# Attention and two feed-forward layers on one core: emission priorities, a longer unordered stretch on ScalarE, and the last output by row blocks

## The chip, the cores and the metric

The kernel runs on one core of a Trainium2 chip. The metric is the time of one execution on the device in microseconds (us), the median of several runs; smaller is better. TensorE (PE in the profile) multiplies matrices, VectorE (DVE) and ScalarE (ACT) work elementwise, GpSimd (POOL) does almost nothing here, and SyncE (SP) issues the transfers (DMAs).

## What is computed

Batch 4, 8 heads, 576 positions, head size 64. Four heads attend to the last 32 positions, four to every 32nd earlier position. The result, 2304 tokens by 512, goes through two feed-forward layers, each 512 to 2048 to 512.

```python
attn = softmax(where(mask, q @ k.T / 8, -1e9))        # heads 0-3: local, heads 4-7: strided
x = (attn @ v).reshape(2304, 512)
h = np.maximum(x @ w_in, 0.0);  x = h * h @ w_out      # first layer
h = x @ w_in2;  g = np.maximum(h, 0) + alpha * np.minimum(h, 0)
out = g @ w_out2                                       # second layer
```

## The kernel before, in words

**Steps.** The two feed-forward layers are a list of 208 steps (layer, tile, f): f counts the 16 blocks of 128 hidden units. Layer 0 has seven tiles of tokens. Tiles 0 to 2 have 256 columns and take steps 0 to 47 (0 to 31 for tiles 0 and 1 in a mixed order, 32 to 47 for tile 2); tiles 3 to 6 have 384 columns and take steps 48 to 111. Layer 1 has six tiles of 384, steps 112 to 207.

**One step.** Every fp32 operand is split into a high part and a low rest, so one product is three products. `emit_h` makes 12 matmuls into one PSUM bank, `ps_h` (line 566). `emit_g` makes the activation on ScalarE: in layer 0 `g` by Relu (L578), `gh`, its square rounded to the short format (L579), and the full square (L580). `emit_gl` subtracts the two on VectorE and gives the rest `gl` (L594). `emit_y` adds 12 matmuls (9 in layer 1) into the output banks `ps_y` (L620): those on `gh` first, those on `gl` last. There is a single `ps_h` bank, so the matmuls of h(n+1) wait until Relu (L578) has read h(n).

**Beside the steps** other work is laid into the list: the conversion of the weights from the 64-bit words in which they arrive (L159, L162, L185 on ScalarE, L171 to L191 on VectorE); the units of local attention (class `Unit`: scores L245, mask and maximum L259 and L263, exponentials L267, scaling L274 to L282, transpose L289 and its copy L293, values L299, output L308 and L315); and strided attention (class `Strided`), which is almost all VectorE work: products L450 and L491, sums L457 and L498. The first two tiles have attention of their own beside (class `Dense`, L340 to L400).

**The order.** Within `run` a step is written as `gl(n)`, h(n+1), attention and conversions, `g(n+1)`, y(n). A framework then orders each engine. Engines named in `manual_schedule` keep the written order; the others get the order in which a scheduler, which estimates when every instruction can start, would pick them by priority, and on the chip each engine then runs its list in that fixed order. SyncE is manual throughout; ScalarE only in the second of two stretches, which begins at step 32. TensorE and VectorE are never manual:

```python
        emit_h(0)
        emit_g(0)
        run(range(2 * NF))
    with tc.manual_schedule(engines={mybir.EngineType.SP, mybir.EngineType.Activation}):
        run(range(2 * NF, len(steps)))
```

**The buffer e.** A unit's masked scores and exponentials lie in `e`, of which there is one for all units from tile 2 on (`bufs=1`, L255). **The end.** `evac` (L625) copies the three output banks of a tile of layer 1 into SBUF, the first and third on ScalarE (L641), the second on VectorE (L643), and SyncE stores each 128 x 512 block (L645).

Of the kernel before, what the change touches and what calls it, by code (L numbers as in the profile page):

```python
# [10 lines left out]
AF = mybir.ActivationFunctionType  # L11
# [5 lines left out]
P = 128  # L17
# [5 lines left out]
NTILE = 6  # L23
# [47 lines left out]
def attn_moe_moe2(  # L71
# [37 lines left out]
    nc = tc.nc  # L109
    NT, DM = out.shape  # L110
    NF = w_in1.shape[0]
    NC = DM // P
    T = NT // NTILE
# [94 lines left out]
    class Unit:  # L208


        bufs = None
# [40 lines left out]

        def softmax_a(self):
            n = self.n
            self.e = self.new("e", [P, 3, 96], bufs=1)[:, 0:n]  # L255
            self.st = apool.tile([P, 3, 4], F32, tag="st", name="stat", bufs=4)[:, :, 0:n]
            s = self.s[:, 0:96 * n].rearrange("p (n c) -> p n c", c=96)
            m = mfirst if self.first else mloc
            nc.vector.scalar_tensor_tensor(  # L259
                out=self.e, in0=s, scalar=SCALE,  # L260
                in1=m.unsqueeze(1).to_broadcast([P, n, 96]), op0=ALU.mult, op1=ALU.add,
            )
            nc.vector.tensor_reduce(out=self.st[:, 0, :], in_=self.e, op=ALU.max, axis=AX.X, negate=True)  # L263
# [284 lines left out]
    steps = [(0, t, f) for t, f in FIRST]  # L548
# [3 lines left out]
    g_sb, y_ps, ybank, hs = {}, {}, {}, {}  # L552
# [38 lines left out]
    def emit_gl(n):  # L591
        g, gh = g_sb[n]
        gl = gpool.tile([P, T], F32R, tag="gl", name="gl")[:, 0:cols_of(n)]
        nc.vector.tensor_tensor(  # L594
            out=gl, in0=g, in1=gh.bitcast(F32), op=ALU.subtract
        )
        g_sb[n] = (gh, gl)

    def emit_y(n):
        l, t, f = steps[n]  # L600
        gh, gl = g_sb.pop(n)
        w = wslot[l, f]
        no = NC if l == 0 else NSUB
        if f == 0:
            for o in range(no):
                if (l, t) != (0, 1):
                    ybank[o] = psum(f"y{o}")
                first = COLS[0] if (l, t) == (0, 1) else 0
                y_ps[l, t, o] = ybank[o][:, first:first + (cols_of(n) if l == 0 else DM)]
        for part in range(2):  # L610
            for o in range(no):
                y = y_ps[l, t, o]
                sl = slice(o * P, (o + 1) * P)
                if l == 0:
                    ops = ((w[:, 2, sl], gh), (w[:, 3, sl], gh), (w[:, 2, sl], gl))
                else:
                    ops = ((gh[:, sl], w[:, 2, :]), (gh[:, sl], w[:, 3, :]), (gl[:, sl], w[:, 2, :]))
                for i, (a, b) in enumerate(ops):
                    if (i == 2) == (part == 1):
                        nc.tensor.matmul(  # L620
                            y, a, b, start=(f == 0 and i == 0 and (l, t) != (0, 1)),
                            stop=(f == NF - 1 and i == 2), skip_group_check=(l == 0 and t < 2),
                        )

    def evac(t, layer):  # L625
        no = NC if layer == 0 else NSUB
        cols = COLS[t] if layer == 0 else DM
        if layer == 0:
            y1[t] = dpool.tile([P, NC, cols], F32, tag=f"y1_{t}", name=f"y1_{t}")
        tags = (("so", 2, 1), ("wt", 2, 2)) if layer == 0 else (("so", 1, 1), ("sq", 1, 1), ("wt", 1, 2))  # L630
        if layer == 0 and t < 2:
            tags = (("wt", 2, 2),) * 2
        evs = []
        for tag, per, bufs in tags:
            ev = spool.tile([P, per, cols], F32, tag=tag, name="ev", bufs=bufs)
            evs += [ev[:, i, :] for i in range(per)]
        for o in range(no):
            ev = evs[o]
            y = y_ps.pop((layer, t, o))
            if o % 2 == 0 or layer == 0:  # L640
                nc.scalar.activation(out=ev, in_=y, func=AF.Copy)  # L641
            else:
                nc.vector.tensor_copy(ev, y)  # L643
            dst = y1[t][:, o, :] if layer == 0 else out[t * T + o * P:t * T + (o + 1) * P, :]
            nc.sync.dma_start(out=dst, in_=ev)  # L645
# [107 lines left out]
    def run(ns):  # L753
        for n in ns:
            l, t, f = steps[n]
            emit(starts, n)
            emit(loads, n)
            emit_gl(n)
            emit(front, n)
            if n + 1 < len(steps):  # L760
                emit_h(n + 1)
            emit(fill, n)
            emit(tensor_part, n)
            if n + 1 < len(steps):
                emit_g(n + 1)
            emit(tail_part, n)
            emit_y(n)
            if f == NF - 1:
                evac(t, l)

    outs = {}
    with tc.manual_schedule(engines={mybir.EngineType.SP}):
# [7 lines left out]
        bufs = {}  # L780
        for t, tags in enumerate((("w7", "w8", "w9", "w10"), ("w15", "w14", "w13", "w12"))):
            n = D * (t + 1)
            a = part(tags[0], 640, 640, 384, 384)
# [55 lines left out]
                fn(*args)  # L839
        emit_h(0)  # L840
        emit_g(0)
        run(range(2 * NF))
    with tc.manual_schedule(engines={mybir.EngineType.SP, mybir.EngineType.Activation}):
        run(range(2 * NF, len(steps)))


_OUTS = [((2304, 512), "float32")]
# [104 lines left out]
```

## Time and profile before

| | us |
|---|---|
| median of 3 runs (894.0 to 895.51) | 895.06 |
| the profiled execution | 895.83 |
| its span, first to last instruction | 894.0 |
| TensorE busy | 870.4 (97%) |
| VectorE busy | 553.5 (62%) |
| ScalarE busy | 455.1 (51%) |

The profiled execution stands 1.8 us above its span. A share over the whole span is a mean over very different stretches: at the start the transfers of weights fill the DMA engines, then VectorE is full with strided attention and weight conversion, and from about 200 us on TensorE has no gap until the last step.

### The profile page before, as it was taken

The numbers are of one execution on the slowest core, as the hardware profiler recorded it, in microseconds if no ns is written. First come the engines' busy times: TensorE is split into PE (matmuls) and PEld (weight loads), VectorE is DVE, ScalarE is ACT, GpSimd is POOL, SyncE is SP. The second block draws the span as 40 slices with busy tenths as digits, with TensorE's granted clock in tenths as the row PEclk, the third lists the DMA queues.
The fourth block names the chain that finished last, engine by engine and source line by source line (L and its number), as shares of the span: only waits on it lengthen the run. The fifth ranks groups of instructions, "written<-read, shape, count | busy, mean of one in ns | idle before, by whom it ended". The sixth has DMA issues, their size and how long they took to land.

```text
span 894.0 us, 13787 instructions
## 1 busy us (share of the span) xinstructions
PE 870.4 (97%) x5448; PEld 817.4 (91%) x5448; DVE 553.5 (62%) x877; ACT 455.1 (51%) x1063; POOL 1.5 (0%) x10
## 2 busy tenths in 40 slices
PE   6799999899999999999999999999999999999997
PEld 5699989799999999999999999999999999999996
DVE  5999999949678796794598983233233333333322
ACT  6889655455545554545577664334334334334332
POOL 0000000000000000000000000000000000000000
PEclk9999999999999999999999999999999999999999
DMA  9990402111212212100687200100100100100000
GB/s 295 393 339 2 153 8 86 45 52 62 71 51 73 68 56 73 49 8 26 241 271 267 82 10 27 36 9 29 34 10 30 33 10 30 33 9 32 5 1 36
DMA packets 33537, 70.34 MB, mean 79 GB/s; under 512 B 5696, under 2 KB 17600, under 8 KB 33472
## 3 DMA queue, kind: packets, MB, share of 16 engines
q1 hardware_dynamic: 33472, 69.46, 22.8%
q8 instruction: 43, 0.70, 0.3%
q14 instruction: 22, 0.18, 0.1%
HBM read 60.01 MB, written 9.44 MB: 78 GB/s over the span
## 4 chain that ended last, share of the span: by engine, by line
PE 88%; DMA 6%; DVE 4%; ACT 1%; issue 1%; SPq 0%; ACTq 0%; DVEq 0%
PE ps_y L620 42%; PE ps_h L566 42%; DMA wraw<-in_w1o_dram 2%; DMA att_w<-in_qd_dram 1%; PE ps_o L299 1%; PE ps_s L245 1%; DMA wraw<-in_w1i_dram 1%; DMA att_w<-in_v_dram 1%; PE ps_pt L289 1%; DVE pr L491 1%; DVE ss L457 1%; DVE w L191 0%; DVE so L498 0%; DVE pr L450 0%; DVE gl L594 0%
## 5 line engine op out<-in xcount | busy, mean ns | idle before, releaser
L566 PE MATMUL ps_h<-xh_c,w 128*128 128x384 f32 (+1 forms) x896 | 221.5, 316 | 4.6 <-ACT g L578 4.2
L566 PE MATMUL ps_h<-xh,w 128*128 128x384 f32 x768 | 212.5, 337 | 0.0
L585 DVE SCALAR_TENSOR_TENSOR g<-u,nalpha,g 128x384 f32<-128x384 f32 x96 | 59.3, 618 | 193.9 <-ACT u L584 193.9
L594 DVE TENSOR_TENSOR gl<-g,gh 128x384 fp32r<-128x384 f32 (+1 forms) x208 | 108.6, 523 | 107.8 <-ACT g L580 57.9
L566 PEld LDWEIGHTS ps_h<-xh_c,w 128*128 128x128 f32 x896 | 157.9, 191 | 7.1 <-ACT g L578 5.4
L620 PE MATMUL ps_y<-gh,w 128*128 128x384 f32 (+1 forms) x896 | 158.3, 319 | 0.0
L620 PE MATMUL ps_y<-w,gh 128*128 128x512 f32 x576 | 149.0, 394 | 0.1
L566 PEld LDWEIGHTS ps_h<-xh,w 128*128 128x128 f32 x768 | 140.4, 188 | 4.2
L566 PE MATMUL ps_h<-xl_c,w 128*128 128x384 f32 (+1 forms) x448 | 140.7, 314 | 0.0
L620 PEld LDWEIGHTS ps_y<-gh,w 128*128 128x128 f32 x896 | 138.7, 190 | 1.5
L583 ACT ACTIVATE g<-ps_h 128x384 f32<-128x384 f32 x96 | 47.2, 492 | 168.5 <-PE ps_h L566 168.2
L566 PE MATMUL ps_h<-xl,w 128*128 128x384 f32 x384 | 128.9, 336 | 0.0
L578 ACT ACTIVATE g<-ps_h 128x384 f32<-128x384 f32 (+1 forms) x112 | 49.4, 441 | 151.2 <-PE ps_h L566 146.6
L620 PEld LDWEIGHTS ps_y<-w,gh 128*128 128x128 f32 x576 | 106.6, 188 | 17.2 <-ACT gh L588 0.6
L620 PE MATMUL ps_y<-gl,w 128*128 128x384 f32 (+1 forms) x448 | 86.2, 313 | 2.0 <-DVE gl L594 1.9
L566 PEld LDWEIGHTS ps_h<-xl_c,w 128*128 128x128 f32 x448 | 85.5, 191 | 0.1
L588 ACT ACTIVATE gh<-g 128x384 fp32r<-128x384 f32 x96 | 50.5, 526 | 68.1 <-DVE g L585 68.1
L620 PE MATMUL ps_y<-w,gl 128*128 128x512 f32 x288 | 82.0, 392 | 0.0
L566 PEld LDWEIGHTS ps_h<-xl,w 128*128 128x128 f32 x384 | 72.1, 188 | 4.1
L620 PEld LDWEIGHTS ps_y<-gl,w 128*128 128x128 f32 x448 | 71.7, 189 | 2.6 <-DVE gl L594 2.6
L620 PEld LDWEIGHTS ps_y<-w,gl 128*128 128x128 f32 x288 | 54.1, 188 | 12.5
L579 ACT ACTIVATE gh<-g 128x384 fp32r<-128x384 f32 (+1 forms) x112 | 53.8, 480 | 2.9
(98 smaller groups left out, 840.7 us busy)
## 6 DMA issues: line engine op xcount, KB each, us to landing
wraw<-in_w1i_dram SPq DMA_DIRECT2D x16, 512.0 KB, 8.8
wraw<-in_w1o_dram SPq DMA_DIRECT2D x16, 512.0 KB, 9.1
wraw<-in_w2i_dram SPq DMA_DIRECT2D x16, 512.0 KB, 3.7
wraw<-in_w2o_dram SPq DMA_DIRECT2D x16, 512.0 KB, 4.7
qk<-in_qk_dram SPq DMA_DIRECT2D x16, 336.0 KB, 3.8
out_dram<-ev SPq DMA_DIRECT2D x18, 256.0 KB, 2.3
y<-ev SPq DMA_DIRECT2D x16, 192.0 KB, 2.0
x2raw<-y SPq DMA_DIRECT2D x16, 192.0 KB, 3.2
```

The source lines that it names most:

```text
L245: nc.tensor.matmul(s, self.qk[:, j, 0:P], self.qk[:, j, P:], start=True, stop=True)
L289: nc.tensor.transpose(self.pt_ps[0:96, P * j:P * j + P], self.e[:, j, :], ident)
L299: nc.tensor.matmul(self.o[64 * h:64 * h + 64, 64 * j:64 * j + 64], self.v[:, j, D * h:D * h + D], self.pt[:, P * j + 64 * h:P * j + 64 * h ...
L457: nc.vector.tensor_reduce(out=self.s[:, b, r:r + ROWS, j0:j1], in_=pr, op=ALU.add, axis=AX.X)
L566: nc.tensor.matmul(h[:, 0:b.shape[2]], a, b[:, c, :], start=(c == 0 and i == 0), stop=(c == NC - 1 and i == 2))
L578: nc.scalar.activation(out=g, in_=h, func=AF.Relu)
L579: nc.scalar.activation(out=gh, in_=g, func=AF.Square)
L583: nc.scalar.activation(out=g, in_=h, func=AF.Relu)
L585: nc.vector.scalar_tensor_tensor(out=g, in0=u, scalar=nalpha[:, f:f + 1], in1=g, op0=ALU.mult, op1=ALU.add)
L588: nc.scalar.activation(out=gh, in_=g, func=AF.Copy)
L594: nc.vector.tensor_tensor(out=gl, in0=g, in1=gh.bitcast(F32), op=ALU.subtract)
L620: nc.tensor.matmul(y, a, b, start=(f == 0 and i == 0 and (l, t) != (0, 1)), stop=(f == NF - 1 and i == 2), skip_group_check=(l == 0 and t ...
```

## The change

Five edits. (1) `e` gets two buffers. (2) `emit_gl(n)` and `emit_g(n+1)` are put under high priority, which the scheduler uses on every engine that it orders. (3) ScalarE's manual stretch begins at step 48 and no longer at step 32, and SyncE's two manual stretches meet there too. (4) In the last step of all, the nine matmuls of y are sorted by output block. (5) In the last tile the second and third output block are copied in two halves, left on VectorE and right on ScalarE, and each half is stored by itself, left from SyncE, right from ScalarE's queue.

```diff
-            self.e = self.new("e", [P, 3, 96], bufs=1)[:, 0:n]
+            self.e = self.new("e", [P, 3, 96], bufs=2)[:, 0:n]
...
-        for part in range(2):
-            for o in range(no):
...
+        order = [(part, o) for part in range(2) for o in range(no)]
+        if n == len(steps) - 1:
+            order.sort(key=lambda x: x[1])
+        for part, o in order:
...
+            if layer == 1 and t == NTILE - 1 and o > 0:
+
+                rows, half = slice(t * T + o * P, t * T + (o + 1) * P), DM // 2
+                nc.vector.tensor_copy(ev[:, 0:half], y[:, 0:half])
+                nc.sync.dma_start(out=out[rows, 0:half], in_=ev[:, 0:half])
+                nc.scalar.activation(out=ev[:, half:], in_=y[:, half:], func=AF.Copy)
+                nc.scalar.dma_start(out=out[rows, half:], in_=ev[:, half:])
+                continue
...
-            emit_gl(n)
+            with tc.high_priority():
+                emit_gl(n)
...
-                emit_g(n + 1)
+                with tc.high_priority():
+                    emit_g(n + 1)
...
-        run(range(2 * NF))
+        run(range(3 * NF))
...
-        run(range(2 * NF, len(steps)))
+        run(range(3 * NF, len(steps)))
```

In the program as built, ScalarE's copy of a right half waits for VectorE's copy of the left half of the same PSUM bank.

Three places show how the order moves; numbers behind names are the framework's, so the same tile may have another one before and after. First VectorE between `gl` of step 25 (`gl_1628`) and of step 26 (`gl_1672`), before:

```order
L594 TENSOR_TENSOR gl_1628<-g_1602,gh_1603 128x256
L457 TENSOR_REDUCE ss_1524<-pr_1587 128x2x5
L315 TENSOR_TENSOR xl_c2_1132<-ps_o_1594,xh_c2_1131 128x128
L450 TENSOR_TENSOR pr_1646<-kv_1440,sq_1482 128x640
L450 TENSOR_TENSOR pr_1648<-kv_1440,sq_1482 128x768
L457 TENSOR_REDUCE ss_1524<-pr_1646 128x2x5
L457 TENSOR_REDUCE ss_1524<-pr_1648 128x2x6
L191 TENSOR_TENSOR w0_15_1630<-wt_1591,w0_15_1630 128x2x512
L594 TENSOR_TENSOR gl_1672<-g_1653,gh_1654 128x256
```

and after the change:

```order
L594 TENSOR_TENSOR gl_1628<-g_1602,gh_1603 128x256
L457 TENSOR_REDUCE ss_1524<-pr_1585 128x2x8
L259 SCALAR_TENSOR_TENSOR e_1608<-ps_s_1599,mloc_79 128x192
L450 TENSOR_TENSOR pr_1587<-kv_1440,sq_1482 128x640
L594 TENSOR_TENSOR gl_1672<-g_1653,gh_1654 128x256
```

Three pieces stand between the two instead of seven; the products, sums and the weight conversion `w0_15` come behind `gl_1672`.

Second ScalarE around steps 36 and 37, before. `g_2095` and `g_2146` are Relu of steps 36 and 37, `e_2058` the second local unit of tile 3, whose exponentials (L267) need the maximum `stat_2059` from VectorE:

```order
L578 ACTIVATE g_2095<-ps_h_2076 128x256
L579 ACTIVATE gh_2096<-g_2095 128x256
L580 ACTIVATE g_2095<-g_2095 128x256
L267 ACTIVATE e_2058,stat_2059<-e_2058,stat_2059 128x96 x3
L282 ACTIVATE e_2058<-e_2058,stat_2059 128x96 x3
L578 ACTIVATE g_2146<-ps_h_2117 128x256
```

and after, where the same unit is `e_2055`, the first unit `e_1957`, and Relu of steps 36 and 37 `g_2092` and `g_2143`:

```order
L267 ACTIVATE e_2055,stat_2056<-e_2055,stat_2056 128x96
L282 ACTIVATE e_1957<-e_1957,stat_1958 128x96 x3
L578 ACTIVATE g_2092<-ps_h_2073 128x256
L267 ACTIVATE e_2055,stat_2056<-e_2055,stat_2056 128x96
L579 ACTIVATE gh_2093<-g_2092 128x256
L267 ACTIVATE e_2055,stat_2056<-e_2055,stat_2056 128x96
L580 ACTIVATE g_2092<-g_2092 128x256
L578 ACTIVATE g_2143<-ps_h_2114 128x256
```

The six instructions that stood between the squares of step 36 and Relu of step 37 are gone from there: the exponentials are spread around step 36, and the scalings L282 of that unit come behind the squares of step 37.

Third ScalarE at step 1, before. `g_470` is Relu of that step, `att_w13_90` the copy of a transpose of dense attention for tile 1, `w0_2` and `wraw` are weight conversion, `xh_c1` the high part of tile 1:

```order
L578 ACTIVATE g_470<-ps_h_453 128x256
L375 ACTIVATE att_w13_90<-ps_pt_491 128x512
L579 ACTIVATE gh_471<-g_470 128x256
L159 ACTIVATE wraw_120<-wraw_120 128x1024
L185 ACTIVATE w0_2_408<-wt_377 128x512 x2
L580 ACTIVATE g_470<-g_470 128x256
L394 ACTIVATE xh_c1_513<-ps_o_412 128x512
```

and after:

```order
L578 ACTIVATE g_470<-ps_h_453 128x256
L267 ACTIVATE att_w15_88,stat_393<-att_w15_88,stat_393 128x96
L579 ACTIVATE gh_471<-g_470 128x256
L267 ACTIVATE att_w15_88,stat_393<-att_w15_88,stat_393 128x96
L580 ACTIVATE g_470<-g_470 128x256
L267 ACTIVATE att_w15_88,stat_393<-att_w15_88,stat_393 128x96 x2
L159 ACTIVATE wraw_120<-wraw_120 128x1024
L185 ACTIVATE w0_2_408<-wt_377 128x512 x2
L375 ACTIVATE att_w13_90<-ps_pt_491 128x512
L394 ACTIVATE xh_c1_513<-ps_o_412 128x512
```

The two squares come earlier; the copy L375 now stands behind them and behind three instructions of weight conversion. The four exponentials L267 stood ahead of `g_470` before.

## Rows read from the trace of the kernel before

**Rows 1.** The page: busy time by engine, and VectorE over 40 slices.

```profile
PE 870.4 (97%) x5448; PEld 817.4 (91%) x5448; DVE 553.5 (62%) x877; ACT 455.1 (51%) x1063; POOL 1.5 (0%) x10
DVE  5999999949678796794598983233233333333322
```

**Rows 2.** Stretches: length, busy PE, PEld, DVE, ACT, POOL, clock, DMA, GB/s.

```profile
111.70:134.00 22.30, 20.64 (x180) 20.04 (x180) 22.14 (x35) 11.20 (x30) 0.00 (x0) 1.00 0.03 8
...
156.00:178.00 22.00, 17.80 (x146) 16.61 (x145) 21.61 (x32) 10.21 (x35) 0.28 (x1) 0.92 0.15 45
...
163.00:166.00 3.00, 3.00 (x24) 2.77 (x23) 3.00 (x5) 1.35 (x5) 0.00 (x0) 0.50 0.02 5
```

**Rows 3.** Waits: who, for whom, us in total, times, longest us.

```profile
PE ps_h L566 <- ACT g L578: 4.2, 1, 4.2
PE ps_y L620 <- DVE gl L594: 1.9, 2, 1.7
ACT e L267 <- DVE stat L263: 4.9, 2, 4.1
```

**Rows 4.** The chain that ended last, 160 to 175 us: start, us, what.

```profile
162.71 2.77 PE ps_h L566 x12
165.47 0.84 PE ps_o L299 x12
...
167.96 1.44 PE ps_h L566 x12
...
172.60 0.50 PE ps_o L299 x12
```

**Rows 5.** Timeline of VectorE ahead of gl of step 26.

```profile
124.14 1.67 DVE L457 TENSOR_REDUCE ss<-pr 128x10 f32<-128x640 f32 x2
125.73 1.22 DVE L191 TENSOR_TENSOR w<-wt,w 128x1024 fp32r<-128x1024 f32 x1
126.86 0.42 DVE L594 TENSOR_TENSOR gl<-g,gh 128x256 fp32r<-128x256 f32 x1
```

**Rows 6.** Timelines of VectorE and ScalarE at the second unit of tile 3.

```profile
158.07 0.44 DVE L263 TENSOR_REDUCE stat<-e 128x3 f32<-128x288 f32 x1
...
158.60 0.37 ACT L267 ACTIVATE e<-e,stat 128x96 f32<-128x96 f32 x1 [4.06 <-DVE stat L263]
...
161.48 0.90 ACT L282 ACTIVATE e<-e,stat 128x96 f32<-128x96 f32 x3 [1.70 <-DVE stat L275]
```

**Rows 7.** VectorE alone over the stretch from gl(24) to gl(47).

```profile
115.90:198.10 82.20, 67.68 (x114) 0.98 0.17 52
```

**Rows 8.** Timelines of ScalarE and TensorE at step 1.

```profile
34.40 0.59 ACT L375 ACTIVATE att_w<-ps_pt 128x512 f32<-128x512 f32 x1
34.87 0.42 ACT L579 ACTIVATE gh<-g 128x256 fp32r<-128x256 f32 x1
...
37.57 0.60 ACT L394 ACTIVATE xh_c<-ps_o 128x512 fp32r<-128x512 f32 x1
...
35.04 1.11 PE L385 MATMUL ps_o<-att_w,att_w 128*32 128x64 f32 x32 [1.07 <-ACT att_w L375]
36.08 1.22 PE L620 MATMUL ps_y<-gh,w 128*128 128x256 f32 x8
...
41.43 0.69 PE L299 MATMUL ps_o<-att_w,att_w 96*64 96x64 f32 x16 [1.58 <-ACT att_w L293]
```

**Rows 9.** Timeline of the end.

```profile
888.14 0.86 PE L620 MATMUL ps_y<-w,gl 128*128 128x512 f32 x3
888.58 1.08 ACT L641 ACTIVATE ev<-ps_y 128x512 f32<-128x512 f32 x2 [1.98 <-PE ps_y L620]
888.81 0.69 DVE L643 COPY ev<-ps_y 128x512 f32<-128x512 f32 x1 [1.61 <-PE ps_y L620]
889.20 1.32 SPq L645 DMA_DIRECT2D out_dram<-ev  x3
```

**Rows 10.** DMA issues, 885 to 894 us and 136 to 148: count, KB, us to landing.

```profile
out_dram<-ev SPq DMA_DIRECT2D x3, 256.0 KB, 2.3
...
y<-ev SPq DMA_DIRECT2D x8, 128.0 KB, 1.8
```

More of the change, by code (lines that the diff above doesn't have):

```diff
@@ L609, in emit_y @@
                 y_ps[l, t, o] = ybank[o][:, first:first + (cols_of(n) if l == 0 else DM)]
-        for part in range(2):
-            for o in range(no):
[L612 to L623, printed above, removed]
+        order = [(part, o) for part in range(2) for o in range(no)]
+        if n == len(steps) - 1:
+            order.sort(key=lambda x: x[1])
+        for part, o in order:
+            y = y_ps[l, t, o]
+            sl = slice(o * P, (o + 1) * P)
+            if l == 0:
+                ops = ((w[:, 2, sl], gh), (w[:, 3, sl], gh), (w[:, 2, sl], gl))
+            else:
+                ops = ((gh[:, sl], w[:, 2, :]), (gh[:, sl], w[:, 3, :]), (gl[:, sl], w[:, 2, :]))
+            for i, (a, b) in enumerate(ops):
+                if (i == 2) == (part == 1):
+                    nc.tensor.matmul(
+                        y, a, b, start=(f == 0 and i == 0 and (l, t) != (0, 1)),
+                        stop=(f == NF - 1 and i == 2), skip_group_check=(l == 0 and t < 2),
+                    )
     def evac(t, layer):
```

## The prediction

> **What bounds the kernel now.** I read the page first: TensorE is busy for 870.4 of 894.0 us, and VectorE's slices stand at 9 from about 45 to 134 us and again before 178 us, then fall [rows 1]. So there are only some 24 us in which TensorE has nothing to do, and the question is which of them the change can reach. A large part lies at the very start, where the first transfers have not landed, and none of the five edits moves those transfers.
>
> The stretches come second. From 111.7 to 134 us TensorE lacks 1.7 us of 22.3; from 156 to 178 us it lacks 4.2 of 22.0, and its granted clock is 0.92 there, 0.50 from 163 to 166 us [rows 2]. VectorE is busy for 22.1 and 21.6 us of the same two stretches: both holes lie where VectorE is full.
>
> The waits say what ended the two holes [rows 3]: one matmul of y waited 1.7 us for `gl`, and one matmul of h waited 4.2 us for Relu, which has to empty the single `ps_h` bank. ScalarE itself waited 4.1 us for a maximum (L263) from VectorE.
>
> The timelines show how each came about. `gl` of step 26 started at 126.86, behind two sums (1.67 us) and a weight conversion (1.22 us) on a VectorE that never paused [rows 5]: it was late because of its place in the queue. The maximum of the second unit of tile 3 started at 158.07; ScalarE, in its written order, had six instructions of this unit ahead of Relu of step 37 and sat idle for 4.06 and 1.70 us before them [rows 6]. TensorE behind it stood still, and when it went on at 162.71, twelve matmuls of h took 2.77 us where the next twelve took 1.44, and twelve of L299 took 0.84 where the later ones took 0.50 [rows 4]. So the idle time was paid again in part: the clock was at 1.2 GHz instead of 2.4 for about 3 us.
>
> **The change, part by part.**
>
> *High priority for gl and g.* Between `gl` of steps 25 and 26 four pieces go behind the second one, among them the conversion of 1.22 us and sums of the kind that take 1.67 us for two [rows 5]; one sum of the step before and the mask L259 come in. On balance `gl` of step 26 moves up by some 6 us of VectorE's list. TensorE missed it by 1.7 us, so this hole closes: -1.7 us. What left the gap is done later by VectorE; nothing waits for it at once, since it belongs to tile 3, whose first step is 48.
>
> *ScalarE unordered in tile 2, with two buffers e.* In the new order the six instructions ahead of Relu of step 37 are gone: the exponentials sit around step 36, their scalings behind the squares of step 37. With the second buffer the mask and maximum of the second unit no longer wait until the first unit is transposed, and in VectorE's new list they stand ahead of `gl` of step 35 instead of behind `gl` of step 36, that is ahead of the products and sums that held them up. So the wait of 4.2 us goes [rows 3], and with it the half clock after it: 2.77 - 1.44 = 1.33 and 0.84 - 0.50 = 0.34, together 1.7 us [rows 4]. Worth -5.9 us. The second buffer alone adds no instruction.
>
> Does VectorE allow this? From `gl` of step 24 to `gl` of step 47 it is busy for 67.7 of 82.2 us [rows 7]. In the new list five more products and sums, of tile 4, stand ahead of `gl` of step 47; at about 0.85 us each, as the two sums of 1.67 us [rows 5], that is 4.3 us. So VectorE has 72.0 us of work in a stretch that is to shrink to 82.2 - 1.7 - 5.9 = 74.6 us. It fits, with 2.6 us to spare: that margin, not TensorE, is what the gain hangs on. What is late next, if it does not fit, is `gl` again. On SyncE's queue the load of the strided values of tile 3 (`kv`) now comes after the eight stores of tiles 0 and 1. Stores of this kind land in 1.8 us [rows 10] and the queue is not crowded there, so I cost the later load at nothing; what hides it is other work in VectorE's list, and if that ran out, VectorE would wait by about such a 1.8 us.
>
> *The first steps.* The priorities reorder these too, and nothing in the trace shows the new order run. One move is plain: the copy L375, needed by the 32 matmuls L385, goes behind the squares of step 1 and three conversions. In the old run these took from 34.87 to 37.57, so the copy comes 2.7 us later [rows 8]. TensorE does y of step 1 in the meantime (1.2 us for its eight matmuls on `gh`, and about 0.3 of its four on `gl`), which it did later before, so it loses 2.7 - 1.5 = 1.2 us. Bounds: at worst the whole 2.7 us is lost; at best `gl` of step 1, which moves up by nearly 9 us of VectorE's list, also lets TensorE use the 1.6 us in which it waited for L299 [rows 8], a gain of 1.5. I take +1.2, since the later copy is a counted row and the gain needs several other things to be early as well.
>
> *The end.* The last matmul ends at 889.0. Then come two copies on ScalarE (1.08 us, from 888.58), one on VectorE, and three stores whose issue starts at 889.20 and takes 1.32 us, 0.44 each [rows 9]; the last one begins at 890.1 and lands 2.3 to 2.5 us later [rows 10]. With the matmuls sorted, the first block is complete about 0.8 us earlier and out of the way; the last block still ends at 889.0. Its left half is copied in about 0.4 us (0.69 for a whole block), issued at 889.5; its right half waits for the left, is copied to about 889.9 and issued at 890.0. So the last issue hardly moves (-0.1), but it is a store of 128 KB, and such stores landed in 1.8 us, 0.5 less than the large ones [rows 10]. That gives -0.6; with the earlier first block a little more: -0.7. The first use of ScalarE's queue is in no row: as cheap as SyncE's 0.44 us, or at worst 1 us dearer, which would eat the gain; so the ends are -0.9 and +0.3.
>
> That the two halves do not run side by side is in the built program: ScalarE waits for VectorE on the same bank. The Trainium skill ("PSUM — Partial Sum Buffer", PSUM bank collisions raise a hardware error) says that two engines must not touch one bank at the same time, so halves of one bank cannot overlap; if they could, the sum for the end would be -1.1. No run here shows a collision.
>
> The Trainium skill ("DMA: Bandwidth & Descriptors", Issuing engines are not separate DMA queues) says that issuing from a second engine saves only the issue time, since all transfers share the same DMA engines. By that rule the two halves of the last block land like one whole block, and the end would give -0.2. No run here has stores from two queues.
>
> *Sum.* -1.7 - 5.9 + 1.2 - 0.7 = -7.1 us. From step 48 on both orders agree where TensorE is concerned, and it has no gap there, so nothing is added. The profiled execution, 895.83, would become 888.7; it stands 0.8 above the median of the runs, so against 895.06 the forecast is **888.0 us**.
>
> **The rivals.**
>
> A. *The wait moves instead of going.* ScalarE's list still has exponentials of the second unit ahead of Relu of step 36, and scalings ahead of others; if VectorE is later than the scheduler thought, one such wait remains. For: VectorE is at 21.6 of 22.0 us there. Against: the maximum is now some 6 us further up in the list, and Relu may be over 1 us late, because TensorE does y of the step before in the meantime. Half of the 5.9 us would stay: 891.0 us.
>
> B. *VectorE is the bound.* If its list from step 24 to step 47 takes all the time it took before, nothing is gained but the end: 894.4 us. Against: it was idle for 14.5 us in that stretch [rows 7].
>
> C. *Slower: gl at the head of the queue before its input is there.* High priority puts `gl` of step 0 ahead of three VectorE instructions which, in the old run, were done while ScalarE was still squaring. An engine works in order, so VectorE stands idle until the square is there, about 1.3 us at that step. In the first 24 steps VectorE is full, so each such wait pushes all later `gl`. If it happens in every step for 0.4 us, that is 10 us, more than the 8.3 us of gains; from 0.35 us per step on the change loses. The price at 0.4 us: 895.06 - 8.3 + 10 = 896.8 us. For: VectorE has few us to spare before 134 us [rows 1]. Against: the wait needs that ScalarE is late in most steps, and after step 12 the new list differs little from the old.
>
> D. *More is gained at the start.* If the order of the first steps gives the 1.5 us instead of costing 1.2: 885.3 us.
>
> **How the numbers follow.** The forecast with its small variations, 886 to 889.5, has 0.55; A 0.22; D 0.08; B 0.07; C 0.08. A difference of under 0.2% (1.8 us) cannot be told from none here. Faster by more: forecast, A, D and the better part of B's neighbourhood, 0.87; within: the rest of B, 0.06; slower: C without its mild cases, 0.07. The range runs from 885.0 (D and the better end of the last stores) to 892.0 (A with the whole 2.7 us lost at the start).
>
> **What would show it.** Right: in the stretch of steps 24 to 47 no wait of h for Relu and none of y for `gl` over 0.5 us, a clock of 1.00 there, and step 48 reached about 6.4 us earlier (7.6 less 1.2); VectorE over 95% busy up to there; the last store landing under 2.9 us after the last matmul. Wrong: a wait of 2 us or more for L578 between 140 and 190 us (A), or VectorE's idle time before 115 us grown by more than 4 us with `gl` as the instruction that waits (C).

## The result and the profile after

| | before | after |
|---|---|---|
| median of the runs measured together, us | 895.28 (894.0 to 903.8, 6 runs) | 888.35 (887.71 to 889.27, 6 runs) |
| span of the profiled execution, us | 894.0 | 887.5 |
| ratio after / before | | 0.9906, 95% interval 0.9879 to 0.9933 |

The forecast was 888.0 us (885.0 to 892.0). Two runs of before at 901.8 and 903.8 us widen the interval; the ratio of the medians is 0.992. Two of the experiments below have a profiled execution with a lower clock over long stretches (`unord_only`, mean granted clock 0.854; `unord_two_e`, 0.50 from 20 to 30 us), so the first is judged by its median alone and the second by its trace from step 4 on.

The steps divide the profiled execution. The table gives the start of the first matmul of h of steps 4 and 48 and the end of the last matmul, from the timelines of TensorE:

| us | before | after | difference |
|---|---|---|---|
| h of step 4 starts | 49.00 | 51.77 | +2.77 |
| from there to h of step 48 | 149.00 | 139.56 | -9.44 |
| from there to the end of the last matmul | 691.0 | 691.4 | +0.4 |
| from there to the end of the span | 5.05 | 4.69 | -0.36 |
| sum | 894.05 | 887.45 | -6.6 |

The +0.4 is of this one execution: a second profile of the same kernel, below, has 690.95. The first row, too, holds more than the change: 0.43 us of it is a later h of step 0 (21.81 and 22.24 us), and four kernels with the same order of instructions up to step 4 (before, `prio_from_4`, `conv_early`, `best_try`) start that step anywhere from 21.8 to 23.4 us. The granted clock differs there as well; the section on the start takes this apart.

The second row by itself, TensorE in that stretch before and after (length, busy PE, clock, DMA share, GB/s):

```profile
49.00:198.00 149.00, 142.72 (x1198) 0.99 0.28 91
51.77:191.33 139.56, 139.47 (x1197) 1.00 0.30 97
```

It is idle for 6.2 us less and busy for 3.2 us less, with the same number of matmuls but for one.

The page of the changed kernel, busy time by engine and VectorE over 40 slices; it answers to [rows 1]:

```profile
PE 866.4 (98%) x5448; PEld 814.4 (92%) x5448; DVE 554.1 (62%) x878; ACT 453.0 (51%) x1064; POOL 1.5 (0%) x10
DVE  5899999996869788793687983233233233233222
```

VectorE does the same work (554 us), but the quiet ninth slice, up to 200 us, is full now (4 before, 9 after): part of what it did after step 48 has moved ahead of it. From `gl` of step 24 to `gl` of step 47, in answer to [rows 7]:

```profile
117.85:191.41 73.56, 71.38 (x118) 1.00 0.25 73
```

The prediction had 72.0 us of work in 74.6 us there.

The stretches of [rows 2], changed kernel (length, busy PE, PEld, DVE, ACT, POOL, clock, DMA, GB/s):

```profile
111.70:134.00 22.30, 22.30 (x194) 21.77 (x194) 22.05 (x39) 12.14 (x33) 0.00 (x0) 1.00 0.03 8
156.00:178.00 22.00, 22.00 (x207) 21.40 (x205) 21.56 (x34) 13.15 (x45) 0.00 (x0) 1.00 0.21 62
163.00:166.00 3.00, 3.00 (x27) 3.00 (x27) 2.88 (x5) 1.99 (x8) 0.00 (x0) 1.00 0.01 3
```

Both holes are gone, and the granted clock is 1.00 (2.4 GHz) where it was 0.50. All that TensorE waited for between 52 and 200 us, where [rows 3] showed 4.2 and 1.9 us:

```profile
PE ps_h L566 <- ACT g L578: 0.8, 1, 0.8
```

and this one wait stands right ahead of h of step 4. So from step 4 to step 48 TensorE is the bound.

The first steps are where the change loses. VectorE and ScalarE of the changed kernel there, to compare with [rows 8] (start, us, what; in brackets the idle time ahead and what ended it):

```profile
27.55 0.69 DVE L172 SCALAR_TENSOR_TENSOR wt<-wraw 128x512 uint32<-128x512 uint32 x1
29.54 0.43 DVE L594 TENSOR_TENSOR gl<-g,gh 128x256 fp32r<-128x256 f32 x1 [1.29 <-ACT g L580]
...
35.60 0.40 ACT L580 ACTIVATE g<-g 128x256 f32<-128x256 f32 x1
36.62 1.15 ACT L159 ACTIVATE wraw<-wraw 128x1024 f32<-128x1024 f32 x1
37.67 1.13 ACT L185 ACTIVATE w<-wt 128x512 fp32r<-128x512 f32 x2
38.71 0.57 ACT L375 ACTIVATE att_w<-ps_pt 128x512 f32<-128x512 f32 x1
```

`gl` of step 0 stands at the head of VectorE's list before its square is there, and VectorE is idle for 1.29 us. The copy L375 stands behind the conversions and starts 4.40 us after Relu of step 1 (34.31); before, it was 0.27 us.

The end, to compare with [rows 9], timeline and then issues (count, KB, us to landing). The edits shift the line numbers: L622 is a matmul of y, L655 the store of the first block, L645 to L648 are the copies and stores of the halves:

```profile
882.12 0.42 DVE L645 COPY ev<-ps_y 128x256 f32<-128x256 f32 x1 [1.17 <-PE ps_y L622]
882.28 0.33 SPq L655 DMA_DIRECT2D out_dram<-ev  x1
882.37 0.39 PE L622 MATMUL ps_y<-w,gl 128*128 128x512 f32 x1
882.58 0.39 ACT L647 ACTIVATE ev<-ps_y 128x256 f32<-128x256 f32 x1 [0.32 <-DVE ev L645]
882.73 0.85 SPq L646 DMA_DIRECT2D out_dram<-ev  x2
882.80 0.42 DVE L645 COPY ev<-ps_y 128x256 f32<-128x256 f32 x1 [0.25 <-PE ps_y L622]
882.99 0.38 ACTq L648 DMA_DIRECT2D out_dram<-ev  x1
883.48 0.38 ACT L647 ACTIVATE ev<-ps_y 128x256 f32<-128x256 f32 x1 [0.52 <-DVE ev L645]
883.89 0.34 ACTq L648 DMA_DIRECT2D out_dram<-ev  x1
```

```profile
out_dram<-ev SPq DMA_DIRECT2D x2, 128.0 KB, 2.2
out_dram<-ev ACTq DMA_DIRECT2D x2, 128.0 KB, 2.4
out_dram<-ev ACTq DMA_DIRECT2D x1, 128.0 KB, 2.6
```

The third row is the last store by itself. It is issued at 883.89 and lands 3.73 us after the last matmul; before, the last store landed 3.58 us after it.

### The profile page after: what moved, and what is told of

The parts are those of the page before. It is cut to its first block, busy times and chain, and to the rows that moved or that the text cites. A ratio compares the mean times of both kernels' runs of the same rounds, so it can differ in the third digit from the quotient of the medians.

```text
span 887.5 us, 13794 instructions
## 1 busy us (share of the span) xinstructions
PE 866.4 (98%) x5448; PEld 814.4 (92%) x5448; DVE 554.1 (62%) x878; ACT 453.0 (51%) x1064; POOL 1.5 (0%) x10
## 3 DMA queue, kind: packets, MB, share of 16 engines
HBM read 60.01 MB, written 9.44 MB: 78 GB/s over the span
## 4 chain that ended last, share of the span: by engine, by line
PE 92%; DMA 5%; ACT 2%; DVE 1%; issue 0%; SPq 0%; ACTq 0%; DVEq 0%
PE ps_h L566 44%; PE ps_y L622 44%; DMA wraw<-in_w1o_dram 2%; DMA att_w<-in_q_dram 2%; PE ps_s L245 1%; PE ps_o L299 1%; DMA wraw<-in_w1i_dram 1%; PE ps_pt L289 1%; ACT wraw L159 0%; ACT att_w L267 0%; DVE g L585 0%; ACT ev L651 0%; DVE w L191 0%; DVE wt L172 0%; ACT wraw L162 0%
## 5 line engine op out<-in xcount | busy, mean ns | idle before, releaser
L585 DVE SCALAR_TENSOR_TENSOR g<-u,nalpha,g 128x384 f32<-128x384 f32 x96 | 59.3, 618 | 192.1 <-ACT u L584 192.1
L622 PE MATMUL ps_y<-gh,w 128*128 128x384 f32 (+1 forms) x896 | 158.3, 318 | 1.4 <-ACT gh L579 1.4
L622 PE MATMUL ps_y<-w,gh 128*128 128x512 f32 x576 | 149.3, 394 | 0.1
L622 PEld LDWEIGHTS ps_y<-gh,w 128*128 128x128 f32 x896 | 137.9, 189 | 2.8 <-ACT gh L579 1.6
L622 PEld LDWEIGHTS ps_y<-w,gh 128*128 128x128 f32 x576 | 106.5, 188 | 17.3 <-ACT gh L588 0.6
L622 PE MATMUL ps_y<-gl,w 128*128 128x384 f32 (+1 forms) x448 | 86.1, 313 | 0.0
L622 PE MATMUL ps_y<-w,gl 128*128 128x512 f32 x288 | 82.3, 392 | 0.0
L622 PEld LDWEIGHTS ps_y<-gl,w 128*128 128x128 f32 x448 | 71.8, 189 | 0.4
L622 PEld LDWEIGHTS ps_y<-w,gl 128*128 128x128 f32 x288 | 54.1, 188 | 12.6
L580 ACT ACTIVATE g<-g 128x384 f32<-128x384 f32 (+1 forms) x112 | 53.6, 479 | 2.8
```

The source lines that it names most:

```text
L580: nc.scalar.activation(out=g, in_=g, func=AF.Square)
L585: nc.vector.scalar_tensor_tensor(out=g, in0=u, scalar=nalpha[:, f:f + 1], in1=g, op0=ALU.mult, op1=ALU.add)
L622: nc.tensor.matmul(y, a, b, start=(f == 0 and i == 0 and (l, t) != (0, 1)), stop=(f == NF - 1 and i == 2), skip_group_check=(l == 0 and t ...
```

## The experiments

Twelve kernels ran, in four groups; the kernels of a group shared one chip and its runs of before. Those vary by up to 10 us, so the ratios have wide intervals, and the traces carry the argument. All step times, for reading along:

| kernel | h(4) | h(48) | h(4) to h(48) | after the last matmul | median | ratio, 95% interval |
|---|---|---|---|---|---|---|
| unord_only | | | | | 891.86 | 0.9938 (0.9905 to 0.9971) |
| unord_two_e | | 198.74 | 143.46 | 5.05 | 891.70 | 0.9937 (0.9913 to 0.9961) |
| prio_only | 51.82 | 193.76 | 141.94 | 4.99 | 890.68 | 0.9927 (0.9897 to 0.9957) |
| prio_from_4 | 49.43 | 190.95 | 141.52 | 4.08 | 887.58 | 0.9878 (0.9836 to 0.9921) |
| after_again | 51.85 | 191.06 | 139.21 | 4.69 | 888.76 | 0.9899 (0.9864 to 0.9934) |
| conv_early | 49.33 | 189.73 | 140.40 | 4.10 | 886.73 | 0.9877 (0.9842 to 0.9912) |
| one_e | 51.79 | 191.09 | 139.30 | 4.68 | 888.89 | 0.9903 (0.9871 to 0.9935) |
| old_end | 52.85 | 192.39 | 139.54 | 4.99 | 889.60 | 0.9907 (0.9871 to 0.9943) |
| gl_only | 50.28 | 190.59 | 140.31 | 4.04 | 887.90 | 0.9896 (0.9851 to 0.9941) |
| g_only | 48.42 | 193.74 | 145.32 | 4.35 | 891.92 | 0.9941 (0.9909 to 0.9974) |
| best_try | 49.28 | 188.41 | 139.13 | 4.29 | 885.57 | 0.9890 (0.9825 to 0.9955) |
| copy_early | 50.99 | 190.39 | 139.40 | 4.69 | 887.87 | 0.9905 (0.9888 to 0.9921) |

**Which edit closes which hole?** My theory was the forecast's: priority closes the hole at step 26, ScalarE's free order the one at step 38. The rivals were that priority closes both, or that the second buffer does it.

`unord_only` is before with edit 3 alone:

```diff
-        run(range(2 * NF))
+        run(range(3 * NF))
...
-        run(range(2 * NF, len(steps)))
+        run(range(3 * NF, len(steps)))
```

> Edit 3 alone (ScalarE ordered by the scheduler up to step 48), no priority, one buffer e, old end. Theory (each hole has its own edit; the hole at step 38 is ScalarE's written order): the exponentials of the second unit of tile 3 now stand behind Relu of step 37, so no wait of h for L578 over 0.5 us and a clock of 1.00 from 156 to 178 us; the hole of 1.7 us at step 26 and the first steps stay as before (h of step 4 at 49.0 us); step 48 reached at 192.1 us instead of 198.0; 889.4 us. Rival 'priority closes both holes': the wait of about 4 us for L578 stays, 895 us. Rival 'the second buffer e does it': with one buffer a wait of 2 us or more stays, 892 us or more.

Its median is 891.86 us, 4.9 us under its runs of before (896.73), against the rival that priority does it all. The 889.4 us of the theory were not reached, and 892 was the other rival's bound, so this run alone doesn't settle the second buffer.

`unord_two_e` is the same with edit 1 (`bufs=2` for `e`).

> Edits 1 and 3 (ScalarE by the scheduler up to step 48, two buffers e), no priority, old end. Theory: within 0.5 us of edit 3 alone, 889.4 us, step 48 at 192.1 us, the hole of 1.7 us at step 26 still there. Rival 'the second buffer does it': 889.4 us here, while edit 3 alone stays at 892 us or more.

Median 891.70, 0.2 us from the run before: the second buffer adds nothing. In its trace the hole at step 26 is there and that at step 38 is nearly gone, as the theory had it. TensorE's waits from 60 to 205 us:

```profile
PE ps_y L620 <- DVE gl L594: 1.9, 2, 1.6
PE ps_h L566 <- ACT g L578: 0.4, 1, 0.4
```

From h(4) to h(48) it takes 143.46 us instead of 149.00, a gain of 5.5. Step 48 itself comes at 198.74 us and not at the 192.1 expected, because this execution was late at the start (h(4) at 55.28, behind 10 us at half clock).

`prio_only` is edit 2 alone:

```diff
-            emit_gl(n)
+            with tc.high_priority():
+                emit_gl(n)
...
-                emit_g(n + 1)
+                with tc.high_priority():
+                    emit_g(n + 1)
```

> Edit 2 alone (high priority for gl and g), ScalarE written out from step 32, one buffer e, old end. Theory: the first steps lose what they lost in the changed kernel (h of step 4 at 51.8 us, +2.8), the hole at step 26 goes (-1.7 to -2.3), and the wait of h of step 38 for Relu of step 37 stays, at 2 to 4.2 us, because the six instructions still stand ahead of it; step 48 at 197 to 199 us, 893 to 896 us. Rival 'priority closes both holes': no wait over 1 us there, step 48 at 192.5 us, 889.5 us.

The start is lost as expected (51.82). But my theory's 2 to 4.2 us at step 38 was wrong, and the rival closer: the wait is 0.88 us, and step 48 comes at 193.76. ScalarE, VectorE and TensorE there, timelines:

```profile
154.15 0.45 DVE L263 TENSOR_REDUCE stat<-e 128x3 f32<-128x288 f32 x1
...
158.00 0.91 ACT L282 ACTIVATE e<-e,stat 128x96 f32<-128x96 f32 x3 [2.19 <-DVE stat L275]
158.81 0.36 ACT L578 ACTIVATE g<-ps_h 128x256 f32<-128x256 f32 x1
...
159.23 0.39 PE L566 MATMUL ps_h<-xh_c,w 128*128 128x256 f32 x1 [0.88 <-ACT g L578]
```

ScalarE still has all six instructions ahead of Relu. But VectorE gives it the maximum (L263) at 154.15 and no longer at 158.07 [rows 6], so most of its wait falls where TensorE has y to do. From step 32 on ScalarE keeps the written order here, so only the priority of `gl` on VectorE can have done this. The two edits overlap: alone each gains 5.5 and 7.1 us between step 4 and step 48, together 9.4.

`one_e` is the whole change with `bufs=1` for `e`.

> The whole change with one buffer e (edit 1 undone). Theory: the second buffer is not needed once ScalarE is not in written order, since the exponentials then stand behind Relu of step 37 anyway; from h of step 32 to h of step 48 52.3 to 53.3 us as in the changed kernel (52.8), time within 0.5 us of after_again. Rival 'the second buffer is what brings the maximum forward': a wait of h for L578 of 1 us or more between 150 and 180 us, that stretch at 54 us or more, at least 1.2 us slower.

Same as `after_again` within 0.13 us. ScalarE's timeline shows why:

```profile
155.70 0.39 ACT L578 ACTIVATE g<-ps_h 128x256 f32<-128x256 f32 x1 [1.59 <-PE ps_h L566]
...
158.25 0.38 ACT L267 ACTIVATE e<-e,stat 128x96 f32<-128x96 f32 x1 [0.98 <-DVE stat L263]
```

With one buffer ScalarE does wait 0.98 us for the maximum, but behind Relu of step 37, where nobody waits for it. Edit 1 is worth nothing beside the others.

`gl_only` and `g_only` are the whole change with one half of edit 2 undone. In `gl_only`:

```diff
-                with tc.high_priority():
-                    emit_g(n + 1)
+                emit_g(n + 1)
```

> The whole change, but high priority for gl alone, not for g. On VectorE gl of step 0 stands at the head as in the changed kernel; on ScalarE the copy L375 of step 1 is back right behind Relu of step 1. Theory of the forecast (the late copy L375 is what costs the start): h of step 4 at 49 to 50 us. Rival (VectorE's wait of 1.29 us with gl of step 0 at the head of its list is passed on through the weight conversions): h of step 4 at 51.2 us or later, as in the changed kernel (51.8). Later: VectorE's list is what closed the holes, so h of step 4 to h of step 48 stays within 1 us of the changed kernel's 139.6 us.

> The whole change, but high priority for g alone, not for gl. ScalarE's copy L375 stands behind the squares and three conversions as in the changed kernel; VectorE's gl of step 0 is back behind three other instructions. Theory of the forecast (late copy L375): h of step 4 at 51 us or later. Rival (VectorE's wait for gl of step 0): h of step 4 at 49 to 50 us. Later: gl of step 26 is late again, a wait of 1 to 1.7 us of y near 125 us; h of step 4 to h of step 48 at 141 to 143.5 us, near the 143.5 us of edits 1 and 3 alone.

Priority for `gl` alone keeps nearly the whole gain of the middle (140.31 against 139.21 to 139.56). With `g` alone it takes 145.32 us, worse than I expected, and the hole at step 26 is larger than before. TensorE's waits in `g_only` from 52 to 200 us:

```profile
PE ps_y L622 <- DVE gl L594: 2.5, 1, 2.5
PE ps_h L566 <- ACT g L578: 0.4, 1, 0.4
```

**Where is the start lost?** The granted clock has to be kept apart first. TensorE from the start of h of step 0 to the start of h of step 4 (length, busy PE, clock, DMA share, GB/s), in before, `best_try`, `g_only`, `copy_early`, `after` (the first profile of the changed kernel), `after_again` and `gl_only`:

```profile
21.81:49.00 27.19, 22.53 (x259) 0.94 1.03 392
23.37:49.28 25.91, 21.17 (x260) 1.00 1.03 390
22.13:48.42 26.29, 21.40 (x259) 1.00 1.03 379
22.54:50.99 28.45, 22.04 (x259) 1.00 1.03 388
22.24:51.77 29.53, 21.61 (x260) 1.00 1.03 383
22.06:51.85 29.79, 22.75 (x259) 0.94 1.03 383
22.06:50.28 28.22, 22.98 (x259) 0.94 1.03 383
```

A mean clock of 0.94 here is one drop to 1.2 GHz for about 3.4 us (in before from 43.5 us on). `best_try` (below) has the order of before up to h(4) and ran without the drop: 25.91 us instead of 27.19. `prio_from_4` and `conv_early`, also in that order and with the drop, take 27.00 and 27.31. So the drop costs 1.1 to 1.4 us in the old order. In the changed order it costs 0.3 us at most: 29.79 and 29.54 with it (`after_again`, `old_end`), 29.53 to 29.58 without. Compared at full clock the change therefore loses 3.6 us at the start (29.53 - 25.91).

In `gl_only` VectorE is idle for 1.31 us ahead of `gl` of step 0, and h(4) starts at 50.28, 1.28 later than before (1.0 counted from h of step 0, both with the drop). That lies between what the two theories of the start gave (49 to 50, and 51.2 or later). In `g_only` h(4) is at 48.42, earlier than before, but at full clock; it is 0.4 us longer than `best_try`. My expectation of `g_only` described it wrongly: in the program as built its copy L375 stands behind the squares, but ahead of the three conversions, so it did not test a late copy. `copy_early` does: the changed kernel with that one copy under high priority.

```diff
-            nc.scalar.activation(out=self.b["pt"], in_=self.pt_ps[0:self.n, :], func=AF.Copy)
+            with tc.high_priority() if (self.t, self.p) == (1, 1) else nullcontext():
+                nc.scalar.activation(out=self.b["pt"], in_=self.pt_ps[0:self.n, :], func=AF.Copy)
```

> The changed kernel, and the copy L375 of step 1 alone under high priority too: on ScalarE it then stands behind the squares of step 1, ahead of the three conversions (L159, L185); beyond step 4 the orders are the changed kernel's. In the run with priority for g alone the copy stood there too, so that run did not test a copy behind the conversions. Theory 'two causes' (1.3 us of the start from VectorE's wait with gl of step 0 at the head, as in the run with gl alone, and the other 1.5 us from the copy behind the conversions): h of step 4 at 50.3 us instead of 51.8, the end 1.5 us earlier or, if VectorE takes it back later, less: 886.8 to 888.3 us. Rival 'VectorE alone' (its delay reaches TensorE through the conversions L191, the copy is hidden): h of step 4 at 51.4 to 51.9 us, 888.3 to 888.8 us.

Lines behind the edit count one more here, so L376 is the copy and L581 the full square; ScalarE's timeline:

```profile
35.89 0.42 ACT L581 ACTIVATE g<-g 128x256 f32<-128x256 f32 x1
...
36.56 0.60 ACT L376 ACTIVATE att_w<-ps_pt 128x512 f32<-128x512 f32 x1
...
37.41 1.17 ACT L159 ACTIVATE wraw<-wraw 128x1024 f32<-128x1024 f32 x1
```

h(4) starts at 50.99, between the two theories: 0.86 us earlier than in `after_again`, and 1.1 counted from h of step 0, against 29.53 to 29.58 us in the kernels with the late copy at full clock. On the same chip, in another group, the median is 887.87 instead of 888.76, 0.9 less. So both causes are there. At full clock the 3.6 us divide like this: 0.4 with priority for `g` (`g_only`), 2.2 more when `gl` has it too and the copy keeps its place (`copy_early`), 1.1 more with the copy behind the conversions (`after`). VectorE's idle time ahead of `gl` of step 0 is 1.3 of the 2.2; the rest I did not take apart.

**Does the lost start cost anything in the end?** `prio_from_4` is the whole change with priority only from step 4 on:

```diff
-            with tc.high_priority():
+            with tc.high_priority() if n >= 4 else nullcontext():
```

(and the same for `emit_g`).

> The whole change, but high priority only from step 4 on, so that the first four steps stand in the order of before. Theory (the priorities of the first steps cost TensorE 2.8 us that nothing later gives back): h of step 4 at 49.0 us as before, step 48 at 191.3 - 2.8 = 188.5 us, 885.6 us. Rival 'VectorE, over 95% busy from 45 to 200 us, sets the end of that stretch, so the delay at the start is hidden': h of step 4 at 49.0 us, but gl late again later, step 48 at 190.5 to 191.3 us, 887.5 to 888.4 us.

The rival was nearer: h(4) is back at 49.43, but step 48 comes at 190.95, 0.4 us before the changed kernel. TensorE's waits from 110 to 145 us, and the first of them in the timeline:

```profile
PE ps_h L566 <- ACT g L578: 0.8, 2, 0.5
PE ps_h L566 <- DVE w L191: 0.8, 1, 0.8
```

```profile
129.50 0.50 PE L566 MATMUL ps_h<-xh_c,w 128*128 128x256 f32 x2 [0.79 <-DVE w L191]
```

The last weight conversion (block 15) stands behind `gl` of step 28 on a full VectorE. Is that its place, or the amount of VectorE's work? `conv_early` also puts L191 of blocks 8 to 15 under high priority, so that it stands behind `gl` of step 25; `after_again` is the changed kernel beside it:

```diff
-        at(fill, n + 1 if layer == 0 else n + 2, convert_d, layer, f)
+        at(fill, n + 1 if layer == 0 else n + 2, hi(convert_d), layer, f)
```

> The changed kernel itself, on the chip of the three runs beside it. Expected as on its own chip: step 32 at about 138.5 us, step 48 at about 191.3 us, last matmul at 882.8 us, 888.3 us.

> As prio_from_4, and the last weight conversion (L191) of blocks 8 to 15 of layer 0 under high priority too, so that the one of block 15, for which TensorE waited at 128 us, stands behind gl of step 25 instead of step 28. Theory 'order': what prio_from_4 won at the start was lost to single pieces in the wrong place; the 1.9 us of waits between 128 and 142 us go, step 32 at 136.2 to 136.6 us, step 48 at 189.0 to 189.4 us, 885.8 us. Rival 'amount': VectorE has so much to do before step 32 that step 32 can't come before about 138 us in any order; other waits take the place, step 32 at 137.7 us or later, step 48 at 190.5 to 191.3 us, 887.5 us.

Step 32, which comes at 137.6 to 139.6 us in the kernels with priority and without this edit, comes at 135.65: the place it was, at least up to there. Then two waits follow, so that step 48 (189.73) falls between the two theories. The waits from 52 to 200 us:

```profile
PE ps_h L566 <- ACT g L578: 0.5, 1, 0.5
PE ps_h L566 <- DVE xl_c L315: 0.4, 1, 0.4
```

The median is 886.73, 2.0 us under `after_again` on the same chip; 0.6 of that comes behind the last matmul (4.10 against 4.69), with the same instructions there.

`best_try` moves that piece too (the low parts of local attention of tile 2), and takes the last blocks whole:

```diff
-        at(fill, n + o[4], unit.emit_lo)
+        at(fill, n + o[4], soon(unit.emit_lo) if unit.t == 2 else unit.emit_lo)
...
-            if layer == 1 and t == NTILE - 1 and o > 0:
...
-                continue
```

> As conv_early, and two more edits: the low parts of local attention of tile 2 (L315) under high priority too, and the last blocks whole, copied and stored as before, with the matmuls of the last step sorted as in the change. First: theory 'order': the waits of 0.39 and 0.47 us at 138 to 141 us go, step 48 at 188.7 to 189.1 us instead of 189.73; rival 'amount of work on VectorE': other waits take their place, step 48 at 189.5 us or later. Second: the DMA engines are full from 0.35 us after the last matmul on, and whole rows moved at 377 GB/s where halves moved at 335; theory 'the transfer sets the end': the last store lands 2.6 to 2.9 us after the last matmul (3.06 in conv_early, 3.73 in the changed kernel, 3.58 before); rival 'the last copy and issue set it': 3.1 us or later. Time by both theories 885.5 us.

No wait of TensorE is left from 52 to 200 us, and step 48 comes at 188.41: theory "order", and slightly better than expected. The median is 885.57 us (one of its four runs took 891.70), 2.3 under `gl_only` on the same chip and the lowest of all kernels here. The second question, too, goes to its theory: the last store lands 2.88 us after the last matmul, within the 2.6 to 2.9 expected.

**The end.** `old_end` is the whole change without edits 4 and 5.

> The whole change with the old end (edits 4 and 5 undone: whole blocks, one copy each, all stores from SyncE). Forecast term of the end: 0.7 us slower from last matmul to the end of the span. From the profile of the changed kernel (4.74 us after the last matmul, 5.05 before) I now expect 5.0 us, 0.3 us slower. Rival 'no gain, the stores land one after the other anyway': 4.7 us as in after_again, or less.

It ends 4.99 us after its last matmul against 4.69, 0.3 us. (Its median is 0.84 above `after_again`, but its profiled execution also started 1.25 us later, so the medians don't measure the end.) Over all kernels the old end takes 4.98 to 5.05 us. The new one takes 4.68 to 4.69 four times (`after`, `after_again`, `one_e`, `copy_early`) and 4.04 to 4.35 four times (`prio_from_4`, `conv_early`, `gl_only`, `g_only`), with the same instructions: in the first group the last store takes 2.6 us to land, in the second 1.9. The DMA rows show one difference. From 2.0 to 3.0 us after the last matmul, in `after` and then in `prio_from_4` (GB/s in 40 slices of 25 ns):

```profile
GB/s 369 287 369 287 451 287 369 287 410 205 410 328 328 287 369 410 246 737 246 451 205 369 205 246 123 123 41 0 0 0 41 41 0 41 0 41 0 41 0 0
q14 instruction: 1, 0.01, 1.9%
```

```profile
GB/s 451 328 328 328 451 246 410 205 451 205 451 246 410 287 369 328 328 410 287 410 287 451 246 247 164 123 82 0 0 0 0 0 0 0 0 0 0 0 0 0
```

In all four profiles of the first group a packet of 8 KB that loads instructions goes out 2.42 to 2.45 us after the last matmul, among the stores (the slice with 737), and behind it the last 1 KB packets of the store (41 in a slice) come singly, until 3.24 to 3.27 us. In the second group that packet comes at 2.92 us or later, and the last data are through at 2.71 to 2.72. That fits the 0.65 us between the landings, eight times out of eight; no run moved this packet by itself, and why it comes earlier in four programs I don't know.

In `best_try`, with sorted matmuls and whole blocks, the end takes 4.29 us. DMA share and GB/s while the engines are full, in `best_try` and in the changed kernel (with the engine column left empty):

```profile
880.50:881.50 1.00, 1.00 1.01 377
```

```profile
883.80:885.10 1.30, 1.00 1.03 337
```

The 16 DMA engines are full in both; whole rows (2 KB) move at 377 GB/s, halves (1 KB) at 337. The halves move more slowly, and their last store lands 3.06 us after the last matmul at best, later than the whole blocks of `best_try` (2.88). The Trainium skill ("DMA: Bandwidth & Descriptors", Issuing engines are not separate DMA queues) says that a second issuing engine saves only the issue time; these rows agree, since the share is near 1 with one issuer and with two.

## Why the prediction was right, point by point

- *gl of step 26.* The hole of 1.7 us is gone, and by the means described: without priority for `gl` it comes back (1.6 us in `unord_two_e`, 2.5 in `g_only`). The count was rough: by the lists seven pieces go behind `gl` of step 26 and three others come in ahead of it, not four out and two in, and VectorE's work ahead of it falls by 5.0 us (113.6 to 108.6), not by some 6.
- *ScalarE unordered, two buffers.* -5.9 us was forecast, and the wait of 4.2 us and the half clock behind it are gone. But the step named one cause too many and missed another. The second buffer does nothing (`one_e`). The free order does close the hole (0.4 us left in `unord_two_e`), but it is not needed for most of it: priority for `gl`, with ScalarE in written order, leaves 0.88 us (`prio_only`). I had read ScalarE's order as the only cause because the six instructions stood there; how long it waits is set by when VectorE delivers the maximum.
- *The middle as a whole.* Forecast -7.6, measured -9.44. Idle time fell by 6.2 us (5.9 of them forecast) and busy time by 3.2, of which the half clock is the 1.7 forecast. The other 1.5 us of busy time are in no single place, at the same number of matmuls; I did not take them apart. VectorE did have the room: it is 97% busy from 45 to 200 us, as forecast (89% before), with 71.4 us of work in 73.6 where 72.0 in 74.6 were forecast, and behind step 4 TensorE never waits for it.
- *The first steps.* This is the step that failed in size: +1.2 forecast, bounds -1.5 to +2.7, measured +2.77, or +2.3 counted from h of step 0, or +3.6 when both orders have the full clock. The largest part was missing: the wait of VectorE for `gl` of step 0 stood, at 1.3 us, only in rival C and not in the sum (measured 1.29), and the priority of `gl` costs 2.2 in all. The copy L375 costs 1.1 by `copy_early`, near the 1.2 taken, but in part by luck: it starts 4.3 us later (34.40 to 38.71) and not 2.7, since the four exponentials L267 ahead of it in the new list were left out of the working, and `copy_early` takes back only 2.4 us of this delay.
- *The end.* Forecast -0.7, measured -0.36 here, up to -1.0 in other kernels. The issues were within 0.1 us of the forecast, and ScalarE's queue is as cheap as SyncE's (0.34 to 0.38 us); the 1 us that the bound allowed for it is in no run. The failing term is the landing: I took 1.8 us for 128 KB from stores that had the DMA engines nearly to themselves; here the last one takes 2.6 with the load of instructions among the stores and 1.9 without, and it lands later than before (3.73 us after the last matmul, where I had named 2.9 as the sign of being right). For the landing the halves are not what helps: with sorted matmuls and whole blocks (`best_try`) the last store lands 0.7 us earlier than before (2.88 against 3.58); the first store is issued 0.7 us earlier there, and the DMA engines are full behind it. The prediction's other sum for the end, -0.2, was nearer.
- *The sum.* -7.1 forecast, -6.6 measured in the profile: +1.6 at the start, -1.8 in the middle, +0.3 at the end and +0.4 in the long stretch behind step 48 nearly cancel. The drop in the clock hides another error: at the start it costs the kernel before 1.1 to 1.4 us, which the forecast did not count, and the profile of the changed kernel has no such cost, so its loss looks that much smaller. The total was right in part by luck, because errors had opposite signs.
- *The rivals.* A and B did not happen. C happened at one step, not in most: no wait of `gl` over 0.4 us follows, and VectorE's idle time before 115 us grows by 1.1 us (13.3 to 14.4), not by the 4 named. D did not happen in any run: `g_only` is 0.9 us shorter than before from h of step 0 to h of step 4, but at full clock, and 0.4 longer than `best_try`.

## What to carry to other kernels

A priority moves an instruction to the head of an in-order engine's list whether or not its input is there: give it from the point on where the engine that feeds it is ahead, and look for the pieces it pushes back (here a weight conversion and an output of attention), for they are the next waits. When one engine waits for another behind a written order, ask first who is late; bringing the late result forward can be worth as much as freeing the order. Two edits that each close most of a hole don't add. Before subtracting two profiles, compare the granted clock of the same stretch: a drop of 3.4 us in one of them stood for 1.1 to 1.4 us here.

## What the runs showed of the hardware that was not expected

- After the last store has landed, the program needs another 1.40 to 1.47 us to its end where SyncE alone issued the stores, as whole blocks (before, `old_end`, `best_try`), and 0.96 to 1.04 where ScalarE's queue issued the last one, a half (1.29 once, in `g_only`). Which of the two differences it hangs on, no run shows. In the changed kernel the gain of 0.36 us at the end is made here, not by an earlier landing (3.73 against 3.58 us).
- What a lower granted clock costs depends on the waits around it. The same drop to 1.2 GHz for 3.4 us cost 1.1 to 1.4 us where TensorE's idle time in the stretch stayed the same (4.7 us in before and in `best_try`), and 0.3 or less where TensorE waited more: in the changed order its busy time grew by 1.1 us (21.61 to 22.75), but its idle time shrank by 0.9 (7.9 to 7.0).
- A load of instructions can fall among the last stores: in four profiles out of four with that 8 KB packet there, the last store landed 0.65 us later than in the four without.
